# A softmax over eight dilated positions: logits copied out of PSUM in bf16, and one more chunk whose tiles are added before the logits

## The chip, the cores and the metric

The kernel runs on one core of one Trainium2 chip. The metric is the device time of one execution in microseconds. Before the change it is 208.17 us, the median of three runs (208.12 to 208.2). The execution that the profiler recorded took 208.24 us, of which the span from its first to its last instruction is 206.1 us.

## The reference

The inputs are a sequence `x` of 2048 rows by 640, and the weights of two branches that both read the normalised `x` and are added to it:

```
xn  = layernorm(x)                                  # no gain, no bias
out = x + A(xn) + B(xn)

A: q, k, v = xn @ wqkv, as 32 heads of 20
   row s looks at rows s, s-2, s-4, ... s-14        # W = 8 positions, dilation 2
   logits = q . k[those rows] / sqrt(20);  -1e9 where the row would be before 0
   o = softmax(logits over the 8) weighted sum of v[those rows]
   A = o @ wo
B: gelu(xn @ w1 + b1) @ w2 + b2                     # hidden width 1536
```

All inputs and the output are bf16.

## The kernel before, in words

The 2048 rows are taken as four chunks of 512 rows (chunk 0 to 3). Everything is kept with features on the partitions and rows along the free dimension, so a chunk of q, k or v is five tiles (t = 0 to 4) of 128 features by 512 rows.

For each chunk:

- ScalarE (ACT) or VectorE (DVE) normalise the rows (`xn`), and TensorE or a transposing DMA turns them (`tp`/`tc`).
- TensorE projects q, k and v (`hj` in chunk 0, `pj` in the others: five matmuls of 512 columns for each tile) and ACT copies each result out of PSUM (`hc`, `pc`). All projections and the first layer of branch B (`f1`) take their PSUM banks from one pool of four buffers, `psA`. A matmul group can begin only when the buffer it gets was emptied by ACT.
- VectorE multiplies q with the shifted k (`qk`, L429) for the eight positions, in two half tiles of four positions each (`half[0]`, `half[1]`), a chunk in four instructions: pair (of 256 rows) by half.
- The 20 products of a head have to be added. TensorE does that with a matrix of zeros and ones, `head_of` (`lg`, L475), in groups of four matmuls, one for each 128 rows, each of which fills 32 of the 128 partitions of `L`. How much VectorE adds beforehand is set by `LEVEL`: at 0 all five feature tiles go to TensorE (40 matmuls), at 1 VectorE first adds tiles 1 and 3 to tiles 0 and 2 (`pa`, L461, four instructions for a chunk) and 24 matmuls are left, at 3 `pb` (L466) adds the rest and 8 are left. Before, `LEVEL = (1, 0, 3, 3)` for the four chunks.
- Softmax (`PARTS` says that chunk 0 is done in two halves of 64 columns, a and b): `m` takes the maximum of the eight positions straight from PSUM (L516), `mx` subtracts it (L522, in f32), `ex` takes the exponential on ACT into the bf16 tile `e` (L532), `ss` adds the eight by halving (4+4, 2+2, 1+1, in f32; L536 and L538), `ri` takes the reciprocal on ACT by a logarithm and an exponential, `at` multiplies (L550) with the f32 reciprocal. In chunk 0 a mask is added first (L486).
- DMAs on the SyncE (SP) queue spread the weights from 32 heads to the partitions (`xd`, `xs`, L569); VectorE weights v (`av`, L584) and adds the eight (`ad`, `ot`).
- TensorE multiplies with w2 and wo (`t` pieces 0 to 3 for w2 and 4 for wo in chunks 0 to 2; `o` in chunk 3), ACT empties (`u`), SP turns (`ut`) and GpSimd (POOL) adds the result to `out` in HBM with an accumulating DMA (`ud`). The rows of `x` themselves are written to `out` before (`xp`, L298): chunk 0 from SP, chunks 1 and 2 from ACT. For chunk 3 they are added on VectorE (`xl`, `dl`, `dh`).

ACT needs one table set for the exponential and the logarithm and another for gelu; every switch is an instruction (L170).

The order of the work on TensorE, VectorE, ACT and SP is written out by hand: `ORDER` lists the pieces by the names above, and each engine runs its own pieces in that order and waits only for the data and the buffers that a piece needs. A name is read as kind, chunk, and the rest: `pj113` is chunk 1, k (0 is q, 2 is v), tile 3; `qk011` chunk 0, pair 1, half 1; `pa011` chunk 0, half 1, columns 256 to 511; `f10_7` chunk 0, tile 7; `t004` chunk 0, output tile 0, part 4. A PSUM buffer that was released earlier in `ORDER` is taken again by a later piece.

Of the kernel before, what the change touches and what calls it, by code (L numbers as in the profile page):

```python
# [37 lines left out]

ORDER = """
pad01 pad02 st00a st00 sum1 rs00 mean1 neg1 sq1 xn00a xn00b tp00a wa tp00b wb tc00a tc00b rs01 ga xn01a xn01b gb2  # L40
tp01a gb3 tp01b tc01a tc01b gb4 gd gc0 ge hj101 st02a tb st03a st02 rs02 st03 ho xn02 tp02 rs03 xn03 b1 st10a st12a
st11a st13a st12 st13 gc4 gc1 tc02 tp03 tc03 hj100 hc100 hj102 st11 hc101 hc102 pk hj010 hc010 hj112 st10 rs1 hc112
rc1 xn12 qk000 xn10 hj111 hc111 tc12 tc10 hj011 hc011 hj201 hc201 hj110 hj012 qk001 hc012 hc110 qk010 xn11 tc11 xn13
pa000 hj210 hj202 hc202 hj200 tc13 hc210 ldx ld2 ldo hc200 f10_0 f10_7 ge0_7 f10_10 f10_4 pj113 ge0_4 ge0_0 pj112
pj104 qk011 ge0_10 pc104 pj111 pc113 pa010 pc111 pa001 pj103 pc112 pa011 lg0 mask m0a mx0a pad11 pc103 su22 ex0a pj100
pc100 pj102 pc102 m0b mx0b ex0b ss0a ri0a ss0b pj114 pc114 at0a ri0b pj101 pc101 at0b xs0 xd0 pj110 pc110 qk100 qk101
qk110 f10_2 ge0_2 f10_9 hj212 su23 hc212 f10_1 qk111 su20 ge0_1 f11_0 ge0_9 su21 ge1_0 ng2 f10_5 f10_6 ge0_6 f11_5
ge1_5 sq23 ge0_5 f11_10 hj211 hc211 f10_3 pj121 lg1 av020 xp0 ge1_10 m1 sq21 ge0_3 av000 pj120 sq22 sq20 rs2 rc2 t040
t041 mx1 pc120 av010 xn22 av001 pc121 xn23 ex1 t000 pj123 tc22 av021 tc23 av031 av011 av030 ss1 f10_11 pj122 pc122
ad00 t001 f10_8 ge0_8 xn21 tc21 f11_9 ge0_11 xn20 tc20 pc123 t002 f11_2 xp1 t042 t043 f11_7 ge1_2 ge1_7 f11_8 ge1_9  # L50
ri1 at1 xp2 pad12 ad01 ad02 ot0 pj124 pc124 t003 pj211 pc211 su33 pj223 pc223 pj212 pj202 pc212 xd1 av111 su30 pj201
av110 pc201 av100 av101 pc202 su32 pj214 pc214 pj224 xs1 av121 av120 av131 pc224 av130 pj204 pc204 pj203 t004 su31
t044 u00 ng3 pad21 u04 t030 sq32 pj213 sq30 sq31 sq33 rs3 rc3 pc213 t031 t032 t033 t010 t011 t012 t013 ut00 ud00 pj200
pc200 t014 u01 pj210 pc210 xn31 tc31 t020 xn33 tc33 pc203 f12_8 t021 ge2_8 pad22 ad11 t022 t023 t034 u03 ad10 xn32
t024 ad12 ot1 f12_9 xn30 ge2_9 f12_11 pj222 pc222 qk201 qk200 qk211 f11_1 ge2_11 ge1_1 f11_3 qk210 tc32 f12_3 ge1_3
tc30 pj300 pc300 pj302 pc302 ut01 ud01 u02 f11_4 ge1_4 pj312 ge2_3 pa211 t100 pa201 pj322 pc322 ge1_8 pa200 pj310
pc310 pj314 pa210 pc312 pj303 pad31 pc303 pj304 pj320 pc314 pc320 pj313 pc313 pj311 pc311 f11_6 pj301 ge1_6 f13_4 t101
pb202 t102 pb212 pb204 pb214 lg2 ut02 f13_7 pc304 pc301 qk300 ge3_7 ut03 f11_11 m2 pa300 ge1_11 mx2 f13_1 ge3_1 t103
t104 u10 ex2 qk311 ss2 ri2 pa311 f13_10 t120 t121 at2 pj221 pc221 f13_8 ge3_4 qk310 t122 t123 t124 t140 t141 t142
ge3_8 f12_7 u12 pj321 pc321 pj324 pc324 xs2 xd2 ge3_10 qk301 ut04 ut10 pj220 t110 t143 f13_0 ge3_0 t111 f12_5 pj323  # L60
ge2_5 f12_10 pc220 ud02 pc323 pa301 pa310 pb302 pb312 pb304 pb314 f13_5 lg3 ge2_10 av220 ud10 f13_11 pad32 ge3_11
ge3_5 m3 mx3 t112 t113 t114 av210 ex3 t144 ss3 u11 av230 f12_0 ut11 ut12 ri3 at3 av201 f13_9 av231 av200 f12_2 t130
ge3_9 u14 t131 ud03 ge2_7 ge2_2 av221 av211 t132 t133 f13_2 ge3_2 f13_6 o300 ge2_0 t134 ad21 ud04 ad20 f13_3 ge3_3
ad22 f12_4 ge2_4 ot2 xd3 av311 f12_1 ge2_1 f12_6 t210 u13 ut13 ge2_6 xs3 av330 av300 ud11 ut14 ud12 ud13 o320 o321
ge3_6 o322 t200 t211 t201 t202 o301 o302 t203 t204 u20 ut20 ud20 av331 t212 t213 t214 t220 o310 u21 ut21 t221 t222
t223 t224 u22 ut22 o311 t230 av310 o312 o313 av301 ud21 ud22 t231 t232 t233 av321 av320 ad30 t234 o303 u23 ut23 t240
t241 t242 t243 t244 u24 o330 o331 o332 o333 ad31 o323 ad32 ot3 o324 o314 o304 xl0 o334 ohi xl1 dl2 ud14 dh2 dl1 dh1
dl0 dh0 ut24 ud23 dl3 dd1 dd2 dd0 dlo dh3 ud24 dhi
""".split()


# [1 line left out]
def kernel(  # L73
# [221 lines left out]

    def do_xp(n):
        cs, dst = rows(n)
        (nc.scalar if n else nc.sync).dma_start(dst, x_sb[:, cs, :])  # L298
# [197 lines left out]
    scratch = half[0][:].rearrange("p w t c -> p (w t c)").bitcast(F32)

    def shifted(n, i):
        if PARTS[n] == 1:
            return tiles["L", n][:]  # L500
        return scratch[:, 0 : W * P].rearrange("p (i w c) -> p i w c", i=PARTS[n], w=W)[:, i, :, :]
# [4 lines left out]
    def sums(n, i):

        if PARTS[n] == 1:
            return attn_tile(n)[:].rearrange("p w c -> p (w c)").bitcast(F32).rearrange("p (w c) -> p w c", w=W // 2)
        room = scratch[:, W * P : W * P + W * P // 2]  # L510
        return room.rearrange("p (i w c) -> p i w c", i=PARTS[n], w=W // 2)[:, i, :, :]

    def do_max(n, i):
        cs, width = part(n, i)
        m = softmax_tile("m", n, [P], F32)
        nc.vector.tensor_reduce(  # L516
            out=m[:, i, :], in_=tiles["L", n][:, :, cs].rearrange("p w c -> p c w"), axis=AX.X, op=ALU.max
        )

    def do_sub(n, i):  # L520
        cs, width = part(n, i)
        nc.vector.tensor_tensor(  # L522
            out=shifted(n, i),
            in0=tiles["L", n][:, :, cs],
            in1=tiles["m", n][:, i, :].unsqueeze(1).to_broadcast([P, W, width]),
            op=ALU.subtract,
        )

    def do_exp(n, i):
        e = softmax_tile("e", n, [W, P], BF16)  # L530
        table(LOG_SET)
        nc.scalar.activation(e[:, i, :, :], shifted(n, i), ACT.Exp, scale=SCALE)  # L532

    def do_sum(n, i):
        a, e = sums(n, i), tiles["e", n][:, i, :, :]
        nc.vector.tensor_tensor(out=a, in0=e[:, 0 : W // 2, :], in1=e[:, W // 2 :, :], op=ALU.add)  # L536
        for k in (2, 1):
            nc.vector.tensor_tensor(out=a[:, 0:k, :], in0=a[:, 0:k, :], in1=a[:, k : 2 * k, :], op=ALU.add)  # L538
# [311 lines left out]
```

## Time and profile before

| | before |
|---|---|
| median of 3 runs (lowest, highest) | 208.17 us (208.12, 208.2) |
| the profiled execution, and its span | 208.24 us, 206.1 us |
| TensorE matmul (PE), busy | 201.9 us, 98% of the span, 1148 instructions |
| VectorE (DVE), busy | 187.1 us, 91%, 162 instructions |
| ScalarE (ACT), busy | 125.0 us, 61%, 228 instructions |
| GpSimd (POOL), busy | 20.9 us, 10% |
| granted TensorE clock | 1.0 |
| DMA | 22.90 MB, mean 111 GB/s |

A busy share is an average over the span; whether an engine sets the time is read from the chain of work that ended last and from the waits. Matmuls overlap each other, so the length of one (379 ns for 512 columns) is not what it adds to the time.

### The profile page before, as it was taken

Reading aid. Unit: us, or ns where it says so; the run is one execution under the profiler, and the core shown is the slowest. Engines: PE = TensorE matmul, PEld = TensorE weight load, DVE = VectorE, ACT = ScalarE, POOL = GpSimd, SP = SyncE. Lnnn points to the kernel's source line nnn. Section 1 sums busy time; section 2 is a strip of 40 time slices with the busy share of each in tenths; the row PEclk is TensorE's granted clock in tenths of the full one; section 3 lists DMA queues with packets and bytes.
Section 4 is the critical chain, followed back from the end, with each engine's and each line's share of the span. In section 5 each row is a group of like instructions: output and inputs, shape, how many; then the busy total and the mean of one; then the engine's idle time right before and its main releaser. Section 6 shows DMA issues by size and latency. Waiting matters only on the chain.

```text
span 206.1 us, 2934 instructions
## 1 busy us (share of the span) xinstructions
PE 201.9 (98%) x1148; PEld 106.2 (52%) x1148; DVE 187.1 (91%) x162; ACT 125.0 (61%) x228; POOL 20.9 (10%) x33
## 2 busy tenths in 40 slices
PE   8999999999999999999999999999999999999994
PEld 3899654545444554444455544444444454444452
DVE  2989995998799999999999969999799999999953
ACT  5688959999897977859655536563488360211100
POOL 2000000000000000200014000001304002332220
PEclk9999999999999999999999999999999999999999
DMA  6996499194026281404437100066706619495543
GB/s 210 392 397 182 74 361 410 57 194 135 0 64 191 101 194 39 50 1 67 91 35 75 17 3 0 0 99 156 54 0 90 114 32 138 51 81 54 56 53 127
DMA packets 36063, 22.90 MB, mean 111 GB/s; under 512 B 24914, under 2 KB 33874, under 8 KB 36050
## 3 DMA queue, kind: packets, MB, share of 16 engines
q1 hardware_dynamic: 26752, 19.24, 34.8%
q0 software_dynamic: 7920, 1.97, 14.0%
q10 hardware_dynamic: 1378, 1.51, 2.0%
q8 instruction: 9, 0.15, 0.3%
q14 instruction: 4, 0.03, 0.1%
HBM read 10.00 MB, written 4.59 MB: 71 GB/s over the span
## 4 chain that ended last, share of the span: by engine, by line
PE 96%; DMA 1%; ACT 1%; DVE 0%; issue 0%
PE T L687 27%; PE hps L605 25%; PE pps L332 24%; PE gps L376 7%; PE lo L643 5%; PE L L475 2%; PE both L643 2%; PE gps L345 1%; PE hi L643 1%; DMA x_sb<-in_A_x_dram 1%; PE tp L277 1%; ACT trash L218 0%; DVE xn L262 0%; ACT logv L242 0%; DVE half L655 0%; ACT rstd L245 0%
## 5 line engine op out<-in xcount | busy, mean ns | idle before, releaser
L605 PE MATMUL hps<-xnT,w_sb 128*128 128x512 bf16 x240 | 55.9, 379 | 0.0
L429 DVE TENSOR_TENSOR half<-qT,kT 128x5120 bf16<-128x5120 bf16 x16 | 44.4, 2819 | 2.3 <-PE L L475 2.0
L687 PE MATMUL T<-hT,w_sb 128*128 128x512 bf16 x180 | 43.4, 379 | 0.0
L605 PEld LDWEIGHTS <-w_sb 128*128 128x128 bf16 x240 | 23.3, 98 | 27.9 <-issue 0.8
L699 POOL DMA_DIRECT2D out_dram<-x_sb x15 | 19.4, 1329 | 177.3 <-DMA x_sb<-x_sb 176.3
L687 PEld LDWEIGHTS <-w_sb 128*128 128x128 bf16 x180 | 17.4, 98 | 20.4
L621 ACT ACTIVATE hT<-hps,bT 128x512 bf16<-128x512 f32 x36 | 24.0, 687 | 6.3 <-PE hps L605 6.3
L584 DVE TENSOR_TENSOR half<-vT,ax 128x2560 bf16<-128x2560 bf16 x16 | 23.0, 1483 | 2.9 <-ACT trash L225 1.6
L690 ACT ACTIVATE x_sb<-T,bT 128x512 bf16<-128x512 f32 x15 | 10.3, 686 | 25.0 <-PE T L687 25.0
L584 DVE TENSOR_TENSOR half<-vT,x_sb 128x2560 bf16<-128x2560 bf16 x16 | 22.6, 1482 | 0.0
L593 DVE TENSOR_TENSOR half<-half,half 128x5120 bf16<-128x5120 bf16 x8 | 22.3, 2820 | 0.1
L332 PE MATMUL pps<-xnT,wv_sb 128*128 128x512 bf16 x75 | 18.3, 379 | 0.0
L687 PE MATMUL T<-oT,wo 128*128 128x512 bf16 x75 | 18.1, 379 | 0.0
L332 PE MATMUL pps<-xnT,wk_sb 128*128 128x512 bf16 x75 | 18.1, 379 | 0.0
L332 PE MATMUL pps<-xnT,wq_sb 128*128 128x512 bf16 x75 | 17.9, 379 | 0.0
L170 ACT ACT_TABLE_LOAD x12 | 15.4, 1283 | 0.9 <-PEq L834 0.7
L461 DVE TENSOR_TENSOR half<-half 128x2048 bf16<-128x2048 bf16 x12 | 14.1, 1217 | 0.0
L396 ACT CAST qT<-pps 128x512 bf16<-128x512 f32 x15 | 8.4, 582 | 7.4 <-PE pps L332 7.4
L332 PEld LDWEIGHTS <-wv_sb 128*128 128x128 bf16 x75 | 8.7, 118 | 7.8 <-issue 0.4
L332 PEld LDWEIGHTS <-wq_sb 128*128 128x128 bf16 x75 | 8.7, 118 | 7.7 <-issue 0.4
L332 PEld LDWEIGHTS <-wk_sb 128*128 128x128 bf16 x75 | 8.8, 117 | 7.5
L396 ACT CAST vT<-pps 128x512 bf16<-128x512 f32 x15 | 8.6, 582 | 6.2 <-PE pps L332 6.1
(94 smaller groups left out, 234.6 us busy)
## 6 DMA issues: line engine op xcount, KB each, us to landing
w_sb<-in_B_w_dram SPq DMA_DIRECT2D x4, 960.0 KB, 10.7
ax<-attn SPq DMA_DIRECT2D x8, 256.0 KB, 4.9
x_sb<-attn SPq DMA_DIRECT2D x8, 256.0 KB, 4.7
out_dram<-x_sb POOLq DMA_DIRECT2D x15, 128.0 KB, 3.9
x_sb<-in_A_x_dram SPq DMA_DIRECT2D x1, 1280.0 KB, 7.4
out_dram<-x_sb ACTq DMA_DIRECT2D x2, 640.0 KB, 3.2
wq_sb<-in_A_wqkv_dram SPq DMA_DIRECT2D x1, 800.0 KB, 4.8
wk_sb<-in_A_wqkv_dram SPq DMA_DIRECT2D x1, 800.0 KB, 6.7
```

The costliest lines, as they stand in the source:

```text
L170: nc.scalar.preload_act_table_set(name)
L332: nc.tensor.matmul(ps[:], lhsT=wqkv_p[which][:, ti, to, :], rhs=xnT[:, ti, :], start=(ti == 0), stop=(ti == KT - 1),)
L376: nc.tensor.matmul(ps[:, to - a, :], lhsT=wqkv_p[which][:, ti, to, :], rhs=tiles["xnT", 0][:, ti, pair * 2 * P : (pair + 1) * 2 * P], star ...
L396: nc.scalar.copy(dest[:, to, off : off + CH], tiles["pps", n, which, to][:])
L429: nc.vector.tensor_tensor(out=half[h][:, :, :, cs], in0=q[:, :, at].unsqueeze(1).to_broadcast([P, W // 2, KT, 2 * P]), in1=window(k, h, at ...
L584: nc.vector.tensor_tensor(out=half[h][:, :, :, cs], in0=window(qkv_tile(n, 2), h, cs), in1=ax_view(n)[:, j, ws, :].unsqueeze(2).to_broadca ...
L593: nc.vector.tensor_tensor(out=a, in0=a, in1=b, op=ALU.add)
L605: nc.tensor.matmul(ps[:], lhsT=w1_sb[:, ti, ft * P : (ft + 1) * P], rhs=tiles["xnT", n][:, ti, :], start=(ti == 0), stop=(ti == KT - 1),)
L621: nc.scalar.activation(hT, tiles["hps", n, ft][:], ACT.Gelu_apprx_tanh, bias=bT[:, ft : ft + 1], scale=1.0)
L643: nc.tensor.matmul(out_ps(bl, hi), lhsT=lhs, rhs=rhs[:, CH:D] if hi else rhs[:, 0:CH], start=pc == 0 and k == 0, stop=pc == 4 and k == len ...
L687: nc.tensor.matmul(ps[:], lhsT=lhs, rhs=rhs, start=pc == 0 and k == 0, stop=pc == 4 and k == len(srcs) - 1)
L699: nc.gpsimd.dma_start(dst, src, accum_op=ALU.add)
```

## The change

- `LEVEL` becomes (1, 1, 3, 3): chunk 1 gets four `pa` instructions on VectorE, and its logits 24 matmuls instead of 40.
- New pieces `cp` copy the logits from PSUM to the bf16 tile `e`: in chunk 0 columns 0 to 63 on ACT (`cp0a`) and 64 to 127 on VectorE (`cp0b`), in chunks 1 to 3 positions 0 to 3 and 4 to 7 (`cp1a`, `cp1b` and so on), both on ACT.
- The mask, the maximum (now by halving, three instructions), the subtraction and the weighting read and write bf16 in SBUF; the exponential works in place on `e`; the reciprocal is stored in bf16. The sum stays in f32.
- All three `xp` are issued from SP; in the new order they stand before `xs0` (`xp0`) and behind `xd0` (`xp1`, `xp2`).
- `ORDER` is another one throughout.

```diff
-LEVEL = (1, 0, 3, 3)
+LEVEL = (1, 1, 3, 3)
...
     def do_xp(n):
         cs, dst = rows(n)
-        (nc.scalar if n else nc.sync).dma_start(dst, x_sb[:, cs, :])
+        nc.sync.dma_start(dst, x_sb[:, cs, :])
...
+    def do_cp(n, i):
+        e = softmax_tile("e", n, [W, P], BF16)
+        if PARTS[n] == 1:
+            ws = slice(W // 2 * i, W // 2 * (i + 1))
+            nc.scalar.copy(e[:, 0, ws, :], tiles["L", n][:, ws, :])
+        else:
+            cs, width = part(n, i)
+            (nc.vector.tensor_copy if i else nc.scalar.copy)(e[:, i, :, :], tiles["L", n][:, :, cs])
+
     def do_mask():
-        L = tiles["L", 0]
-        nc.vector.tensor_tensor(out=L[0:H, :, 0:MW], in0=L[0:H, :, 0:MW], in1=mask[:], op=ALU.add)
+        e = tiles["e", 0][0:H, 0, :, 0:MW]
+        nc.vector.tensor_tensor(out=e, in0=e, in1=mask[:], op=ALU.add)
+
+    def fold(a, e, op):
+        nc.vector.tensor_tensor(out=a, in0=e[:, 0 : W // 2, :], in1=e[:, W // 2 :, :], op=op)
+        for k in (2, 1):
+            nc.vector.tensor_tensor(out=a[:, 0:k, :], in0=a[:, 0:k, :], in1=a[:, k : 2 * k, :], op=op)
 
     def do_max(n, i):
-        nc.vector.tensor_reduce(
-            out=m[:, i, :], in_=tiles["L", n][:, :, cs].rearrange("p w c -> p c w"), axis=AX.X, op=ALU.max
-        )
+        fold(room(n, i, BF16, 0), tiles["e", n][:, i, :, :], ALU.max)
 
     def do_sub(n, i):
...
-            out=shifted(n, i), in0=tiles["L", n][:, :, cs],
-            in1=tiles["m", n][:, i, :].unsqueeze(1).to_broadcast([P, W, width]), op=ALU.subtract,
+        e = tiles["e", n][:, i, :, :]
+        m = room(n, i, BF16, 0)[:, 0, :].unsqueeze(1).to_broadcast([P, W, width])
+        nc.vector.tensor_tensor(out=e, in0=e, in1=m, op=ALU.subtract)
 
     def do_exp(n, i):
-        nc.scalar.activation(e[:, i, :, :], shifted(n, i), ACT.Exp, scale=SCALE)
+        nc.scalar.activation(e, e, ACT.Exp, scale=SCALE)
 
     def do_sum(n, i):
+        fold(room(n, i, F32, W // 2 * P), tiles["e", n][:, i, :, :], ALU.add)
 
     def do_recip(n, i):
-        rs = get(("rs", n), lambda: smp.tile([P, PARTS[n], P // PARTS[n]], F32, tag="m", name="rs"))
+        rs = softmax_tile("rs", n, [P], BF16)
```

The part of the new `ORDER` from the logits of chunk 0 to those of chunk 1 and somewhat on:

```
... lg0 pc112 su20 cp0b cp0a m0b mask pj111 mx0b ex0b m0a pj114 pc114 ss0b mx0a pj101 pc101 ri0b pj113 pc113 ex0a pc111
pj100 at0b pc100 ss0a su22 qk111 ri0a qk101 pj124 pc124 at0a qk110 pa111 qk100 pa110 pa101 f11_3 pa100 f11_10 ge1_3 ldo
f10_8 ge0_8 hj210 hc210 xp0 su21 f10_2 ge0_2 su23 ge1_10 f10_0 ng2 ge0_0 f10_7 f10_3 f10_4 sq22 ge0_3 ge0_7 f11_5 sq21
ge0_4 sq23 f10_6 ge0_6 pj121 xs0 sq20 rs2 t040 t041 f11_0 rc2 pj122 pc122 xn22 pc121 xd0 xp1 xp2 tc22 xn23 tc23 lg1 cp1a
f10_10 f11_1 ge1_1 ge1_0 xn21 av020 cp1b ge0_10 t000 t001 t042 t002 xn20 f10_9 av030 av000 f11_9 ge1_9 av001 av011 tc21
f11_11 ge0_9 tc20 ge1_5 m1 av021 mx1 ex1 av031 pj120 ...
```

More of the change, by code (lines that the diff above doesn't have):

```diff
@@ L40 @@
 pad01 pad02 st00a st00 sum1 rs00 mean1 neg1 sq1 xn00a xn00b tp00a wa tp00b wb tc00a tc00b rs01 ga xn01a xn01b gb2
[L41 to L68, printed above, removed]
+tp01a gb3 tp01b tc01a tc01b gb4 gd gc0 ge st03a st02a tb hj100 st03 rs03 st02 xn03 b1 rs02 xn02 st11a st13a st10a st13
@@ new lines @@
+st12a st10 st12 st11 gc4 gc1 tp03 tc03 tp02 tc02 ho hj101 hc101 hj102 hc102 hj011 hc100 hc011 rs1 hj112 hc112 rc1 xn12
+tc12 qk000 hj012 qk001 hj201 xn10 tc10 hc012 hc201 hj211 hc211 hj110 hc110 hj010 hc010 f10_1 pk pa000 xn13 hj111 tc13
+xn11 tc11 ldx ld2 pa010 hc111 qk010 hj212 qk011 pa001 pa011 hc212 f10_5 f10_11 ge0_11 ge0_1 hj200 ge0_5 hc200 hj202
+pj103 pc103 pj104 pc104 pad11 pj110 pc110 pj102 pc102 pj112 hc202 lg0 pc112 su20 cp0b cp0a m0b mask pj111 mx0b ex0b
+m0a pj114 pc114 ss0b mx0a pj101 pc101 ri0b pj113 pc113 ex0a pc111 pj100 at0b pc100 ss0a su22 qk111 ri0a qk101 pj124
@@ new lines @@
+pc124 at0a qk110 pa111 qk100 pa110 pa101 f11_3 pa100 f11_10 ge1_3 ldo f10_8 ge0_8 hj210 hc210 xp0 su21 f10_2 ge0_2
+su23 ge1_10 f10_0 ng2 ge0_0 f10_7 f10_3 f10_4 sq22 ge0_3 ge0_7 f11_5 sq21 ge0_4 sq23 f10_6 ge0_6 pj121 xs0 sq20 rs2
+t040 t041 f11_0 rc2 pj122 pc122 xn22 pc121 xd0 xp1 xp2 tc22 xn23 tc23 lg1 cp1a f10_10 f11_1 ge1_1 ge1_0 xn21 av020
+cp1b ge0_10 t000 t001 t042 t002 xn20 f10_9 av030 av000 f11_9 ge1_9 av001 av011 tc21 f11_11 ge0_9 tc20 ge1_5 m1 av021
+mx1 ex1 av031 pj120 pc120 t003 pj123 pc123 t043 pad12 av010 pj221 pc221 ss1 pj224 ri1 ad01 at1 pc224 pj220 pj200 su33
@@ new lines @@
+pc220 ad00 ad02 ot0 pc200 pj214 pc214 xs1 su32 av131 pj202 pc202 pj213 pc213 pad21 pj212 pc212 su31 pj204 pj210 pc210
+pc204 av121 pj211 pj203 pj201 su30 ng3 sq32 sq30 t004 u00 t044 u04 sq31 pc211 xd1 av101 av100 av111 av120 av130 sq33
+ut00 t010 ud00 t011 t012 t013 t014 pc201 av110 u01 rs3 rc3 pj222 pc203 pad22 ad10 t030 t031 f11_6 xn32 tc32 t032 ad11
+ad12 t020 t021 t022 xn30 tc30 f11_2 pc222 ge1_2 t023 t033 t034 xn33 tc33 t024 ge1_6 ot1 f11_4 qk201 qk200 qk210 xn31
+ge1_4 qk211 pa200 pa211 pa201 u03 pa210 pb202 pb212 pb204 pj223 f12_1 pc223 f11_8 ge1_8 f12_6 ut01 ge2_6 ge2_1 pb214
@@ new lines @@
+t130 tc31 pj310 pc310 pj303 pc303 pj301 pc301 ge1_11 f11_7 pj311 pc311 pj302 pj312 pc302 pj313 pc312 ge1_7 pc313 u02
+ut02 pj300 f13_3 f12_10 pc300 pj322 pc322 pj320 pc320 pj304 ge2_10 ut03 ut04 ud01 pad31 pc304 pj314 pc314 ud02 ge3_3
+f13_9 f12_7 ge3_9 ge2_7 lg2 cp2b qk310 cp2a m2 mx2 f13_5 ge3_5 qk311 f13_2 pj324 pc324 pj321 ex2 ss2 pa311 t131 t132
+t133 ri2 at2 xd2 t140 t134 ud03 pc321 u13 ge3_2 f13_7 t141 t142 t143 f13_4 f13_0 t100 ge3_7 t101 f12_11 ge2_11 pj323
+t102 t103 qk300 f13_6 t104 ge3_6 f13_10 ge3_10 ge3_0 t144 u14 f12_0 ge3_4 pc323 ge2_0 qk301 xs2 pa300 pa310 pa301
@@ new lines @@
+pb312 pb302 pb314 f13_1 pb304 lg3 xl0 cp3a cp3b av230 ge3_1 av201 m3 av210 pad32 t110 f12_3 f12_2 t111 t112 mx3 t113
+t114 u10 ut10 ex3 f12_8 f12_9 o300 av200 ss3 u11 ut11 av220 ri3 at3 av231 t120 av211 av221 o301 ud10 t121 t122 ge2_3
+t123 f13_8 ge2_2 ge3_8 ge2_9 ad21 ad20 t124 xd3 xs3 ad22 u12 ut12 ot2 av321 av331 f12_5 f13_11 ge3_11 f12_4 ge2_5 t230
+o310 ge2_4 av320 t231 ge2_8 t232 o320 av330 av311 av300 av310 av301 ad30 t200 ud11 t233 t201 t202 t203 o321 ud04 t204
+ut13 ut14 u20 ut20 t234 ad31 u23 t210 t211 t212 t213 ud12 t214 t220 u21 t221 o322 t222 t223 t224 u22 o311 o330 o312
@@ L69 @@
+ud13 o313 ud20 o302 t240 ut21 t241 t242 t243 o323 t244 o331 o303 o332 o333 ad32 ot3 o324 xl1 o314 o304 dl2 ud14 dh2
+dl1 u24 o334 dh1 dl0 ohi ud21 ut22 ud22 ut23 ut24 dd2 dd1 dh0 dd0 dl3 dh3 dhi dlo ud23 ud24
 """.split()
@@ L482, in do_lg @@
                     )
-    def do_mask():
-        L = tiles["L", 0]
-        nc.vector.tensor_tensor(out=L[0:H, :, 0:MW], in0=L[0:H, :, 0:MW], in1=mask[:], op=ALU.add)
     def part(n, i):
@@ L494, in softmax_tile, with room @@
         return get((key, n), lambda: smp.tile([P, PARTS[n]] + [s // PARTS[n] if s == P else s for s in shape], dtype, tag=key, name=key))
[L496 to L501, printed above, removed]
+    scratch = half[0][:].rearrange("p w t c -> p (w t c)")
     def attn_tile(n):
         return get(("attn", n), lambda: smp.tile([P, W, P], BF16, tag="attn", name="attn"))
-    def sums(n, i):
+    def room(n, i, dtype, off):
+        size = W // 2 * P // PARTS[n] * (2 if dtype == F32 else 1)
@@ L508, in sums @@
         if PARTS[n] == 1:
-            return attn_tile(n)[:].rearrange("p w c -> p (w c)").bitcast(F32).rearrange("p (w c) -> p w c", w=W // 2)
-        room = scratch[:, W * P : W * P + W * P // 2]
-        return room.rearrange("p (i w c) -> p i w c", i=PARTS[n], w=W // 2)[:, i, :, :]
-    def do_max(n, i):
-        cs, width = part(n, i)
-        m = softmax_tile("m", n, [P], F32)
-        nc.vector.tensor_reduce(
-            out=m[:, i, :], in_=tiles["L", n][:, :, cs].rearrange("p w c -> p c w"), axis=AX.X, op=ALU.max
-        )
+            flat = attn_tile(n)[:].rearrange("p w c -> p (w c)")[:, 0:size]
+        else:
+            flat = scratch[:, off + i * size : off + (i + 1) * size]
@@ new lines, in room, with do_mask @@
+        return flat.bitcast(dtype).rearrange("p (w c) -> p w c", w=W // 2)
+    def do_cp(n, i):
[3 more added lines that the diff above has]
+            nc.scalar.copy(e[:, 0, ws, :], tiles["L", n][:, ws, :])
+        else:
+            cs, width = part(n, i)
+            (nc.vector.tensor_copy if i else nc.scalar.copy)(e[:, i, :, :], tiles["L", n][:, :, cs])
+    def do_mask():
+        e = tiles["e", 0][0:H, 0, :, 0:MW]
+        nc.vector.tensor_tensor(out=e, in0=e, in1=mask[:], op=ALU.add)
@@ L520, in do_sub @@
+    def fold(a, e, op):
+        nc.vector.tensor_tensor(out=a, in0=e[:, 0 : W // 2, :], in1=e[:, W // 2 :, :], op=op)
+        for k in (2, 1):
+            nc.vector.tensor_tensor(out=a[:, 0:k, :], in0=a[:, 0:k, :], in1=a[:, k : 2 * k, :], op=op)
+    def do_max(n, i):
+        fold(room(n, i, BF16, 0), tiles["e", n][:, i, :, :], ALU.max)
     def do_sub(n, i):
         cs, width = part(n, i)
[L522 to L527, printed above, removed]
+        e = tiles["e", n][:, i, :, :]
+        m = room(n, i, BF16, 0)[:, 0, :].unsqueeze(1).to_broadcast([P, W, width])
+        nc.vector.tensor_tensor(out=e, in0=e, in1=m, op=ALU.subtract)
@@ L529, in do_exp @@
     def do_exp(n, i):
-        e = softmax_tile("e", n, [W, P], BF16)
+        e = tiles["e", n][:, i, :, :]
         table(LOG_SET)
-        nc.scalar.activation(e[:, i, :, :], shifted(n, i), ACT.Exp, scale=SCALE)
+        nc.scalar.activation(e, e, ACT.Exp, scale=SCALE)
     def do_sum(n, i):
[L535 to L538, printed above, removed]
+        fold(room(n, i, F32, W // 2 * P), tiles["e", n][:, i, :, :], ALU.add)
@@ L540, in do_recip @@
     def do_recip(n, i):
-        rs = get(("rs", n), lambda: smp.tile([P, PARTS[n], P // PARTS[n]], F32, tag="m", name="rs"))
-        total = sums(n, i)[:, 0, :]
+        rs = softmax_tile("rs", n, [P], BF16)
+        total = room(n, i, F32, W // 2 * P)[:, 0, :]
         table(LOG_SET)
@@ L779 @@
         piece(f"lg{n}", do_lg, n)
+        for i in range(2):
+            piece(f"cp{n}" + "ab"[i], do_cp, n, i)
         for name, fn in (("m", do_max), ("mx", do_sub), ("ex", do_exp), ("ss", do_sum), ("ri", do_recip), ("at", do_attn)):
```

## The prediction

> **What bounds the kernel now.** I read the totals, then the chain of work that ended last, then the waits, and only then the prices of single instructions. First the page's own lines (busy times; the ACT row of the 40 slices, in tenths; the chain by engine):
>
> ```profile
> span 206.1 us, 2934 instructions
> ...
> PE 201.9 (98%) x1148; PEld 106.2 (52%) x1148; DVE 187.1 (91%) x162; ACT 125.0 (61%) x228; POOL 20.9 (10%) x33
> ...
> ACT  5688959999897977859655536563488360211100
> ...
> PE 96%; DMA 1%; ACT 1%; DVE 0%; issue 0%
> ```
>
> TensorE is the chain. VectorE is nearly as full, and ScalarE is full in the first 85 us. The chain in order of time (start, length, what) shows that it is not merely busy:
>
> ```profile
> 31.99 1.41 PE L L475 x24
> ...
> 41.08 0.55 PE gps L376 x5
> ...
> 49.19 1.08 PE hps L605 x5
> ...
> 51.35 2.27 PE L L475 x40
> ...
> 62.81 0.65 PE T L687 x3
> ...
> 121.52 0.55 PE L L475 x8
> ...
> 147.64 0.55 PE L L475 x8
> ...
> 202.08 0.96 PE hi L643 x17
> 203.06 0.29 DVE half L655
> ```
>
> From the first projections to 203 us each piece starts where the last one stops; in the waits no PE line of the middle of the kernel appears. Five matmuls of 512 columns add 1.08 us, three 0.65 us, five of 256 columns 0.55 us. So the time is the sum of matmul work plus a start and a tail, and two things count: what TensorE has to do, and whether a new order leaves it waiting.
>
> **TensorE.** Chunk 1's logits go from 40 matmuls to 24. Chunk 0 has run 24 already: 1.41 us against 2.27 us. That removes 0.86 us of the chain; nothing else on TensorE changes in number or shape. (By 16 equal shares of the 2.27 us it would be 0.91 us; I take the row.)
>
> **VectorE.** The rows by shape (the last two numbers before the bar are count and busy time, then the mean ns of one):
>
> ```profile
> L461 DVE TENSOR_TENSOR half<-half 128x2048 bf16<-128x2048 bf16 x12 | 14.1, 1217 | 0.0
> ...
> L522 DVE TENSOR_TENSOR L<-L,m 128x1024 f32<-128x1024 f32 x3 | 3.7, 1226 | 0.0
> L516 DVE TENSOR_REDUCE m<-L 128x128 f32<-128x1024 f32 x3 | 3.7, 1217 | 0.0
> L550 DVE TENSOR_TENSOR attn<-e,rs 128x1024 bf16<-128x1024 bf16 x3 | 3.6, 1217 | 0.0
> ...
> L655 DVE TENSOR_TENSOR half<-lo,x_sb 128x512 bf16<-128x512 f32 x3 | 2.1, 692 | 1.9 <-PE lo L643 1.9
> ...
> L536 DVE TENSOR_TENSOR attn<-e 128x512 f32<-128x512 bf16 x3 | 2.0, 682 | 0.0
> ...
> L302 DVE TENSOR_TENSOR x_sb<-x_sb,b2bc 128x1280 bf16<-128x1280 bf16 x2 | 1.6, 817 | 0.0
> L522 DVE TENSOR_TENSOR half<-L,m 128x512 f32<-128x512 f32 x2 | 1.4, 691 | 0.1
> L550 DVE TENSOR_TENSOR attn<-e,rs 128x512 bf16<-128x512 bf16 x2 | 1.4, 688 | 0.0
> ...
> L538 DVE TENSOR_TENSOR attn<-attn 128x256 f32<-128x256 f32 x3 | 1.3, 425 | 0.1
> ...
> L538 DVE TENSOR_TENSOR attn<-attn 128x128 f32<-128x128 f32 x3 | 0.9, 292 | 0.1
> ...
> L538 DVE TENSOR_TENSOR half<-half 128x64 f32<-128x64 f32 x2 | 0.5, 225 | 0.1
> ```
>
> All-bf16 rows give 2048 elements in 1217 ns and 1280 in 817: 0.52 ns for each element and about 150 ns besides. L550 is the telling one: with one f32 operand 1024 elements take those same 1217 ns. So I estimate for all-bf16 operations 684 ns (1024), 417 (512), 284 (256), 217 (128), 183 (64); the upper ends are the f32 rows of equal size.
>
> - Chunks 1 to 3, each: the maximum by halving 417 + 284 + 217 = 918 ns against 1217; the subtraction 684 against 1226; the weighting 684 against 1217. Together 1.37 us less. At f32 prices (682 + 425 + 292 for the halving) 0.2 us more.
> - Chunk 0, each half: halving 284 + 217 + 183 = 684, about what it was; subtraction and weighting 0.27 us less each. Added: `cp0b`, 512 elements out of PSUM, 0.42 to 0.69 us, taken at 0.69 (L655 is nearest).
> - Chunk 1: four `pa`, 4 × 1.217 = 4.87 us more.
>
> In all -4.1 - 1.1 + 0.7 + 4.9 = +0.4 us on VectorE. The total costs nothing by itself; what counts is whether VectorE is in time where TensorE takes its results.
>
> **ScalarE.** Seven copies of 512 columns out of PSUM come on top, at the price of the casts it does now; the 13 instructions of the densest stretch are summed with these rows (time line and groups):
>
> ```profile
> 35.76 1.05 ACT L396 CAST qT<-pps 128x512 bf16<-128x512 f32 x2
> ...
> 39.95 1.28 ACT L170 ACT_TABLE_LOAD   x1
> 41.24 0.69 ACT L621 ACTIVATE hT<-hps,bT 128x512 bf16<-128x512 f32 x1
> ...
> 62.01 0.42 ACTq L298 DMA_DIRECT2D out_dram<-x_sb  x1
> ```
> ```profile
> L621 ACT ACTIVATE hT<-hps,bT 128x512 bf16<-128x512 f32 x36 | 24.0, 687 | 6.3 <-PE hps L605 6.3
> ...
> L260 ACT ACTIVATE xn<-x_sb,nmr,rstd 128x640 bf16<-128x640 bf16 x12 | 10.6, 916 | 0.9 <-DVE nmr L250 0.9
> ...
> L532 ACT ACTIVATE e<-half 128x512 bf16<-128x512 f32 x2 | 1.3, 636 | 0.4 <-DVE half L522 0.4
> ```
>
> Two casts take 1.05 us, so one behind another adds about 0.48; in the same way a gelu adds 0.58, an `xn` 0.82, a table load 1.29. The number of table loads stays. Copies 7 × 0.48 = 3.4 us, less the issue of two transfers (0.42 each), over the whole kernel.
>
> **Where TensorE could wait: the logits of chunk 1.** VectorE now has 4.9 us more ahead of `lg1`, which stands later in the order. VectorE's rows:
>
> ```profile
> 15.62 8.29 DVE L429 TENSOR_TENSOR half<-qT,kT 128x5120 bf16<-128x5120 bf16 x3
> 23.83 1.22 DVE L461 TENSOR_TENSOR half<-half 128x2048 bf16<-128x2048 bf16 x1
> 24.97 2.82 DVE L429 TENSOR_TENSOR half<-qT,kT 128x5120 bf16<-128x5120 bf16 x1
> ...
> 121.94 2.83 DVE L429 TENSOR_TENSOR half<-qT,kT 128x5120 bf16<-128x5120 bf16 x1 [1.99 <-PE L L475]
> ...
> 142.22 4.62 DVE L466 TENSOR_TENSOR half<-half 128x2048 bf16<-128x2048 bf16 x4
> ...
> 172.85 1.49 DVE L598 TENSOR_TENSOR oT<-half 128x2560 bf16<-128x2560 bf16 x1
> ```
>
> A `qk` adds (23.83 - 15.62)/3 = 2.74 us, a `pa` 24.97 - 23.83 = 1.14.
>
> TensorE: ahead of `lg0` stand one `f1` (1.08) and `hj210` (1.10) fewer, `hj211` (1.10) and `hj212` (0.55) more, so `lg0` runs from 31.99 - 0.53 = 31.46 to 32.87. VectorE has chunk 0's four `qk` and four `pa` done at 15.62 + 10.95 + 4.56 = 31.13: no wait. From `lg0` to `lg1` TensorE has 19 groups of 1.08, `hj210` and two of 0.65: `lg1` is due at 32.87 + 20.52 + 1.10 + 1.30 = 55.79.
>
> VectorE from 32.87: `cp0b` to 33.56, `m0b` 34.25, mask 34.47, `mx0b` 34.89, `m0a` 35.57; `ex0b` on ScalarE ends at 34.89 + 0.64 = 35.53, so `ss0b` (425 + 292 + 225 ns) ends at 36.5, `mx0a` at 36.93. Then ScalarE rules: `ex0a` is queued behind `pc113`, whose matmuls end four groups after `lg0`, at 37.19; `pc113` to 37.77, `ex0a` 38.41, and behind it `pc111` and `pc100`, to about 39.5. `ss0a` ends at 39.35, and `qk111` needs `pc100`: 39.5. Four `qk`, four `pa` and `at0a` (0.35): 39.5 + 10.95 + 4.56 + 0.35 = 55.4. Against 55.79 that leaves 0.4 us. At the upper prices `mx0a` ends 1.04 us later, of which 0.84 disappear in the wait for `pc113`; with `at0a` 0.5 us late in all, a wait of 0.1.
>
> **PSUM buffers behind it.** `rc2` stands behind `pa100` on VectorE, and `xn22`, with all of ScalarE's queue, behind `rc2`. From 55.79, when `pj122` ends: `pc122`, `pc121`, `cp1a`, `cp1b` 1.92, four `xn` 3.28, a table load 1.29, `ge1_1`, `ge1_0`, `ge0_10` 1.74, `ge1_9` 0.58: 8.8 us, to 64.6, which frees the buffer that I take `pj120` to get. `pj120` is due after `lg1` (1.41), two `f1`, four `t` parts, three `f1`: 55.79 + 1.41 + 2.16 + 2.60 + 3.24 = 65.2. Cover 0.6 us. `cp1a` waits for `lg1` in that queue, but is reached only after the `lg1` matmuls have ended.
>
> **Later hand-overs.** `lg2` to `lg3`: before, VectorE began 0.42 us after `lg2` (121.94 against 121.52), ended at 146.84 and was 0.8 us ahead of 147.64. After, VectorE has 24.9 - 1.4 = 23.5 us, TensorE thirteen groups of 1.08, eleven of 0.65, three of 1.08 and 0.55, together 25.0: 1.1 us ahead. `ot2` ended at 174.34, ahead of `t204`, for which I count 27.2 us of TensorE work from 147.64: 0.5 us ahead. After, both lose about 1.4 us: the cover is again 0.5. From `ot2` to `ot3` no operation changes.
>
> **SyncE.** `xp1` and `xp2` now stand between `xd0` and the transposes of chunk 2, and `xp0` ahead of `xs0`. SyncE's row:
>
> ```profile
> 43.96 0.60 SPq L298 DMA_DIRECT2D out_dram<-x_sb  x1
> ```
>
> Three times 0.6 us of issue; chunk 0's weights (`at0a` at 45.3) are used after 55.4, and `xn22` isn't there before 57: hidden on both sides by several us, and without that cover 0.6 us each.
>
> **The sum.** The profiled execution's 208.24 us is its span of 206.1 and 2.14 around it; the median is 0.07 lower. 208.17 - 0.86 = **207.3 us** with every wait covered. About 0.2% (0.42 us) is what a measurement of this kernel can tell from no change, so two thirds of the gain must reach the end to be 207.75 or less.
>
> **The rivals.**
>
> 1. *The covers leak (same).* Those I found are 0.4 to 0.6 us, thinner than the errors of sums over twenty rows. Waits of 0.45 to 1.28 us in all give 207.75 to 208.6. For it: ScalarE's nines up to 85 us; against: the order before had covers of 0.5 to 0.8 us and no wait. 0.14.
> 2. *The matmuls removed were free (same).* If the four groups run beside each other so well that 16 fewer save nothing: 208.2. Against it stand 1.41 and 2.27 us in the chain. 0.03.
> 3. *ScalarE becomes the bound between 55 and 66 us (slower).* It is the one place where VectorE's new work, ScalarE's new copies and the PSUM pool meet: everything waits for `rc2`. ScalarE late by d makes TensorE wait d - 0.6 for a buffer at `pj120`. From d = 1.9 (0.6 + 0.86 + 0.42) the kernel is slower; with 0.2 us more for each of its 13 instructions d is 2.6 and the time 209.3. For it: the queue has no idle time in my sum. Against: its rows are those of instructions that run there today. 0.13.
> 4. *The bf16 forms run at one element a cycle (slower).* VectorE then pays 1.55 us more in each of chunks 1 to 3 than I took: waits of 0.1 at `lg1`, 0.45 at `lg3`, 1.05 at `ot2`: 208.9; it decides from about 1.4 us more for each. Against: L461, in place, and L429, with a repeated operand, run at two. 0.05.
> 5. *Table loads drain (same).* If a load cost 1.38 us more than its row, ScalarE would be that late at `pj120`, and the time 207.3 + 0.8 = 208.1. The rows say no: the gelu starts 1.29 us after its load began. 0.02. The Trainium skill's "ScalarE: Activation LUTs" ("What ACT_TABLE_LOAD costs") states a drain of about 1380 ns behind the load's 1283 ns; the trace has the 1283 and not the drain, so by that rule the kernel would land at rival 5, and I don't follow it.
>
> **How the numbers follow.** The forecast has 0.63; rivals 1, 2 and 5 make "same" 0.19, rivals 3 and 4 "slower" 0.18. The range begins at 207.0 (0.3 under the forecast, for 0.91 in place of 0.86 and the scatter of single pieces) and reaches over the "same" cases to 208.6, leaving out the slower 0.18.
>
> **What would show it.** Right: `L` in chunk 1 as 24 matmuls in about 1.4 us; no idle time of PE before L332, L475 or L687; L550's successor near 684 ns; VectorE's total within 1 us of 187. Wrong: PE waiting for ACT in front of projections near 65 us (rival 3), or for DVE in front of `L` or of the first `T` part with wo (rivals 1 and 4).

## The result, and the profile after

| | before | after |
|---|---|---|
| median, first comparison | 208.16 us (4 runs) | 207.1 us (4 runs, 206.87 to 207.37) |
| ratio, 95% interval | | 0.9949 [0.9932, 0.9967] |
| ratio of a second comparison, on its own chip | | 0.9948 [0.9935, 0.9960], median 206.98 us |
| profiled execution, its span | 208.24 us, 206.1 us | 207.11 us, 205.2 us |

The kernel is 0.5% faster, 1.06 us by the medians; 207.3 us was forecast. The page after, lines as shown of before:

```profile
span 205.2 us, 2907 instructions
...
PE 199.6 (97%) x1113; PEld 105.5 (51%) x1132; DVE 187.2 (91%) x177; ACT 127.8 (62%) x235; POOL 20.9 (10%) x33
...
ACT  5689967999899887859655576571775650211100
...
PE 95%; DMA 1%; ACT 1%; issue 1%; DVE 0%
```

VectorE's total moved by 0.1 us although four additions came on, ScalarE's by 2.8. TensorE is still the chain. TensorE's own total can't be compared here: 1113 of the 1132 matmuls that run are in this trace (a second one, of the same kernel, has all 1132 and 201.3 us), and the pieces whose records are missing make up the "issue 1%". The chain in order of time, at the places shown of before:

```profile
31.44 1.41 PE L L475 x24
...
55.87 1.41 PE L L475 x24
...
65.37 1.08 PE pps L332 x5
...
123.64 0.55 PE L L475 x8
...
148.69 0.55 PE L L475 x8
...
201.18 0.96 PE hi L645 x17
202.17 0.29 DVE half L657
```

Chunk 1's logits take 1.41 us in place of 2.27, and the last matmul group begins at 201.18 in place of 202.08: 0.90 us earlier, the 0.86 and next to nothing else. The rest of the 1.06 us, some 0.2 to 0.3, lies outside the span (see the last point on the prediction). In the list of waits no PE line names another engine for the middle of the kernel. The new VectorE instructions by shape (mean ns behind the comma):

```profile
L532 DVE TENSOR_TENSOR e<-e,attn 128x1024 bf16<-128x1024 bf16 x3 | 2.1, 687 | 0.0
...
L552 DVE TENSOR_TENSOR attn<-e,rs 128x1024 bf16<-128x1024 bf16 x3 | 2.1, 684 | 0.0
...
L521 DVE TENSOR_TENSOR attn<-e 128x512 bf16<-128x512 bf16 x3 | 1.3, 421 | 0.0
...
L523 DVE TENSOR_TENSOR attn<-attn 128x256 bf16<-128x256 bf16 x3 | 0.9, 292 | 0.1
...
L523 DVE TENSOR_TENSOR attn<-attn 128x128 bf16<-128x128 bf16 x3 | 0.7, 225 | 0.1
```

Each is within 10 ns of its estimate (684, 684, 417, 284, 217); the copy of 512 elements out of PSUM took 0.69 us, in a row shown further down.

### The profile page after: what moved, and what is told of

Read it like the earlier page. It is cut to its first block, busy times and chain, and to the rows that moved or that the text cites. A ratio compares the mean times of both kernels' runs of the same rounds, so it can differ in the third digit from the quotient of the medians.

```text
span 205.2 us, 2907 instructions
## 1 busy us (share of the span) xinstructions
PE 199.6 (97%) x1113; PEld 105.5 (51%) x1132; DVE 187.2 (91%) x177; ACT 127.8 (62%) x235; POOL 20.9 (10%) x33
## 4 chain that ended last, share of the span: by engine, by line
PE 95%; DMA 1%; ACT 1%; issue 1%; DVE 0%
PE T L689 27%; PE hps L607 25%; PE pps L332 24%; PE gps L376 7%; PE lo L645 5%; PE both L645 2%; PE L L475 2%; PE hi L645 2%; PE gps L345 1%; DMA x_sb<-in_A_x_dram 1%; PE tp L277 1%; ACT trash L218 0%; DVE xn L262 0%; ACT logv L242 0%; DVE half L657 0%
## 5 line engine op out<-in xcount | busy, mean ns | idle before, releaser
L607 PE MATMUL hps<-xnT,w_sb 128*128 128x512 bf16 x232 | 55.3, 379 | 0.4
L689 PE MATMUL T<-hT,w_sb 128*128 128x512 bf16 x179 | 42.7, 379 | 0.1
L461 DVE TENSOR_TENSOR half<-half 128x2048 bf16<-128x2048 bf16 x16 | 18.8, 1219 | 0.0
L260 ACT ACTIVATE xn<-x_sb,nmr,rstd 128x640 bf16<-128x640 bf16 x12 | 10.7, 918 | 2.9 <-DVE nmr L250 2.2
```

What stands on the lines that cost most here:

```text
L461: nc.vector.tensor_tensor(out=even, in0=even, in1=odd, op=ALU.add)
L607: nc.tensor.matmul(ps[:], lhsT=w1_sb[:, ti, ft * P : (ft + 1) * P], rhs=tiles["xnT", n][:, ti, :], start=(ti == 0), stop=(ti == KT - 1),)
L689: nc.tensor.matmul(ps[:], lhsT=lhs, rhs=rhs, start=pc == 0 and k == 0, stop=pc == 4 and k == len(srcs) - 1)
```

## The experiments

Three groups of kernels ran, each on its own chip beside runs of the kernel before (medians 208.12, 208.3 and 208.27 us); between groups the ratios are to be compared. Theory A throughout: the gain is the 16 matmuls, and everything else in the change makes room for VectorE's four additions without letting TensorE wait.

**The changed kernel again.**

> The changed kernel itself, as an anchor for the others of this chip: 207.1 us by every theory (its runs so far 206.9 to 207.4), and TensorE's last matmul near 202.1 us as in its first profile.

206.98 us, ratio 0.9948, the span again 205.2 us: the anchor holds.

**Chunk 1 back at level 0.**

```diff
-LEVEL = (1, 1, 3, 3)
+LEVEL = (1, 0, 3, 3)
```
with `pa100`, `pa101`, `pa110`, `pa111` out of `ORDER`.

> The changed kernel with chunk 1 at level 0: no adds ahead of its logits and 40 matmuls; order, bf16 softmax and x writes as changed. Theory A (the gain is the 16 matmuls, everything else only keeps TensorE from waiting): 0.86 us above the changed kernel, 207.95, and VectorE's 4.6 us less buy nothing. Theory B (the gain comes from the new order or the softmax): no difference, 207.1.

207.78 us, ratio 0.9981 [0.9972, 0.9990]: 0.80 us above the changed kernel. Its chain:

```profile
55.93 2.27 PE L L475 x40
...
202.10 0.96 PE hi L645 x17
```

The matmuls are what the span lost: with them back, the last group begins at 202.10, against 202.08 in the kernel before. Against B. But the time is still 0.34 us below the kernel before with the same span of 206.1 us; that remainder is followed below.

**The old softmax in the new order.**

On the kernel before:

```diff
-LEVEL = (1, 0, 3, 3)
+LEVEL = (1, 1, 3, 3)
-        (nc.scalar if n else nc.sync).dma_start(dst, x_sb[:, cs, :])
+        nc.sync.dma_start(dst, x_sb[:, cs, :])
```
with the new `ORDER` without the `cp` pieces.

> The changed kernel with the old softmax: maximum and subtraction in f32 straight from PSUM, no copies; level 1 in chunk 1, the new order without the copies, x writes from SyncE. Theory A (VectorE must be in time, and its covers are 0.2 us at chunk 1's logits, 1.0 at chunk 2's, 0.85 at chunk 3's, 0.5 at the attention output of chunk 2): 1.4 us more on VectorE for each of chunks 1 to 3 make TensorE wait about 0.1 + 0.5 + 0.5 + 0.9 us: 209.1. Theory B (VectorE has room, the bf16 softmax isn't needed): 207.1.

208.62 us, ratio 1.0027 [1.0016, 1.0038]: slower than before, with 16 matmuls fewer. Its time lines, TensorE and then VectorE:

```profile
55.78 1.48 PE L475 MATMUL L<-half,head_of 128*32 128x512 bf16 x24
...
123.55 0.79 PE L475 MATMUL L<-half,head_of 128*32 128x512 bf16 x8
...
149.15 0.61 PE L475 MATMUL L<-half,head_of 128*32 128x512 bf16 x8 [0.31 <-DVE half L466]
...
175.93 2.32 PE L687 MATMUL T<-oT,wo 128*128 128x512 bf16 x10 [0.83 <-DVE oT L598]
```
```profile
119.27 4.62 DVE L466 TENSOR_TENSOR half<-half 128x2048 bf16<-128x2048 bf16 x4
124.06 2.83 DVE L429 TENSOR_TENSOR half<-qT,kT 128x5120 bf16<-128x5120 bf16 x1 [0.17 <-PE L L475]
...
174.39 1.49 DVE L598 TENSOR_TENSOR oT<-half 128x2560 bf16<-128x2560 bf16 x1
```

The waits stand at chunk 3's logits and at the first product with chunk 2's attention output, as theory A had it. At chunk 2's logits a small one lies inside the group: VectorE's last addition ends at 119.27 + 4.62 = 123.89, after the group has begun, and the eight matmuls take 0.79 us where the changed kernel's take 0.62. At chunk 1's logits there is none: without the copies VectorE began its multiplications for chunk 1 at 39.42, 0.35 us earlier than with them. Against the changed kernel TensorE is 0.16 us late behind chunk 2's logits, 0.53 at chunk 3's (149.15 against 148.62 in the same view) and 1.53 at the attention output (175.93 against 174.40): about 1.5 us and not 2.0; the medians differ by 1.64. The bf16 softmax is needed, although alone it is worth nothing (next but two).

**The x writes back on ScalarE.**

```diff
-        nc.sync.dma_start(dst, x_sb[:, cs, :])
+        (nc.scalar if n else nc.sync).dma_start(dst, x_sb[:, cs, :])
```

> The changed kernel with the writes of x for chunks 1 and 2 issued by ScalarE again, at their new place in the order. Theory A (the move from ScalarE to SyncE is worth nothing): 207.0 to 207.2. Theory B (two issues of 0.42 us land in ScalarE's full stretch at 57 us, where a PSUM buffer comes free 0.3 us before TensorE needs it): up to 0.5 us more, 207.6.

207.19 us, ratio 0.9959 [0.9945, 0.9972] beside 0.9948 [0.9935, 0.9960]. The intervals overlap: if the move is worth anything it is some 0.2 us, which the times don't resolve. The chain in its trace shows where they come from:

```profile
57.34 4.58 DMA xnT<-xn
...
62.01 0.55 ACT xn L260
...
64.80 0.59 ACT hT L623
...
65.43 1.24 PE pps L332 x5
66.67 0.65 PE T L689 x3
```

The two issues (0.42 and 0.52 us) cost ScalarE nothing: they run beside its other work, and the normalisation behind the first begins at 56.40, against 56.39 in the changed kernel. But now the two writes of 640 KB move while chunk 2 is transposed. One transposing DMA lands after 4.6 us, where all four of the changed kernel take 2.4, ScalarE waits 0.34 us for it (until 62.01), and the gelu that frees `pj120`'s buffer ends at 65.39. TensorE takes the buffer at 65.43: the cover there is just used up, and what follows stands 0.22 us later (66.67 against 66.45). So theory B has the place and less than half of the size, but not the reason.

**The kernel before, once more.**

> The kernel before, unchanged, for a second profile of it: the changed kernel with 40 matmuls ended its span with the same 206.1 us as the first profile of the kernel before, and yet was 0.34 us faster in the comparison. Theory A (the 0.3 us lie outside the span and belong to single executions): span 206.1, and a time less span below the 2.14 us of the first profile. Theory B (the kernel before has a longer time outside its span): 2.1 us again.

Ratio 1.0009 [0.9982, 1.0036], as it should be. The profiled execution took 209.46 us with a span of 207.3 us; outside the span lie 2.16 us, as 2.14 in the first profile, and 2.1 to 2.2 us in all twelve executions. So theory B, in numbers. That span was longer for a reason at its very start:

```profile
1.20 6.28 DMA wq_sb<-in_A_wqkv_dram
...
7.53 1.03 PE gps L345 x15
...
203.31 0.96 PE hi L643 x17
```

The first weights landed late (6.3 us after their issue, 4.8 in the first profile), TensorE began its projections at 7.53 us, and everything up to the end was shifted by 1.2 us. A single execution of this kernel can differ by more than the change is worth, for a transfer in its first 8 us.

**The bf16 softmax alone, in the old order.** The new functions with `LEVEL = (1, 0, 3, 3)`, x writes from ScalarE, and the copies put into the old order where ScalarE is free:

```diff
-lg0 mask m0a mx0a pad11 pc103 su22 ex0a
+lg0 pad11 pc103 su22 cp0b cp0a mask m0a mx0a ex0a
-m1 sq21 ge0_3 av000 pj120 sq22 sq20
+sq21 ge0_3 av000 pj120 sq22 sq20 cp1a cp1b m1
...
```
with `cp2a cp2b` behind `pc301` and `cp3a cp3b` behind `pad32`.

> The kernel before with the bf16 softmax alone: its own order, with the copies put where ScalarE reaches them, level 0 in chunk 1, x writes from ScalarE as before. Theory A (TensorE doesn't wait in the kernel before, so a faster softmax on VectorE buys nothing): 208.0 to 208.2. Theory B (the softmax itself shortens the time): 207.6 or less. A third way: the two copies of chunk 1 wait for the logits in ScalarE's full queue ahead of the next normalisation: up to 1 us slower, 209.1.

208.49 us, ratio 1.0005 [0.9990, 1.0020]: no change, though VectorE was busy 183.2 us instead of 187.1. Two things cancel in this: the span of the profiled execution is 0.7 us longer than before (206.8 us), and the time outside it 0.3 us shorter (1.8 us in all executions). In the trace TensorE has one new wait, 0.36 us at 43.15 for a gelu on ScalarE. It isn't the third way: the chain that leads there begins with the copies of chunk 0, not of chunk 1 (`cp0b` at 33.54, `cp0a` behind it at 34.26, the mask at 34.88).

**The four additions alone, in the old order.**

```diff
-LEVEL = (1, 0, 3, 3)
+LEVEL = (1, 1, 3, 3)
-... f10_3 pj121 lg1 ...
+... f10_3 pj121 pa100 pa101 pa110 pa111 lg1 ...
```

> The kernel before with level 1 in chunk 1 alone: the four adds put in VectorE's order ahead of the logits, everything else as before. Theory A (the adds have to be hidden by an order with later logits): VectorE ends its multiplications 0.4 us before the logits are due, the adds take 4.6 us, so TensorE waits 4.2 us, gets 0.86 back and waits some 0.5 us more for the attention output of chunk 0: 212.0. Theory B (TensorE has slack there, the matmuls removed are the whole of it): 207.3.

210.99 us, ratio 1.0152 [1.0105, 1.0199], about 3 us slower: theory A's direction, less than its 3.9 us by the median (the interval reaches from 2.2 to 4.1 us). The profiled execution is one of the long ones, 212.38 us with a span of 210.5; four of the six took 210.74 to 211.14. The time line shows the logits of chunk 1 following the additions one at a time:

```profile
52.11 0.39 PE L475 MATMUL L<-half,head_of 128*32 128x512 bf16 x2 [0.83 <-DVE half L461]
53.25 0.82 PE L475 MATMUL L<-half,head_of 128*32 128x512 bf16 x10 [0.74 <-DVE half L461]
54.38 0.39 PE L475 MATMUL L<-half,head_of 128*32 128x512 bf16 x2 [0.31 <-DVE half L461]
55.52 1.47 PE L475 MATMUL L<-half,head_of 128*32 128x512 bf16 x10 [0.74 <-DVE half L461]
```

**The new order alone.** The kernel before with the new `ORDER`, from which the `cp` and the `pa1` pieces are taken out.

> The kernel before in the new order alone: old softmax, level 0 in chunk 1, x writes from ScalarE, the copies and the four adds left out of the order. Theory A (the new order hides work and shortens nothing): the 0.86 us of matmuls are back and the waits for the old softmax at the logits of chunk 3 and the attention output of chunk 2 stay as they were with 24 matmuls, 0.45 and 0.9 us: 209.2. Theory B (the new order by itself is worth 0.3 us): 207.8.

209.85 us, ratio 1.0064 [1.0040, 1.0089]: the order by itself makes the kernel 1.3 us slower by the ratio (1.1 expected), with VectorE late at the same places as under the old softmax:

```profile
PE T L687 <- DVE oT L598: 0.8, 1, 0.8
...
PE L L475 <- DVE half L466: 0.5, 1, 0.5
```

None of the three parts helps alone: +1.3 us, nothing, +3 us. Together they take 1 us away.

**VectorE made late.** In the changed kernel, one addition that nothing uses:

```diff
+    def do_xx(n):
+        nc.vector.tensor_tensor(out=spare[:], in0=half[0][:, :, n, :], in1=half[0][:, :, n, :], op=ALU.add)
-... pa101 f11_3 pa100 ...
+... pa101 f11_3 xx1 pa100 ...
```

> The changed kernel with one more VectorE instruction (an addition of 2048 bf16 elements that nothing uses, 1.22 us, 1.14 in a row) just ahead of the last add before the logits of chunk 1. Theory A (the cover there is the 0.2 us of the trace, and what exceeds it reaches the end): 0.95 us above the changed kernel, 207.95. Theory B (VectorE is busy 91% and so has room, a later wait takes it up): 207.0 to 207.1.

Ratio 0.9999 [0.9984, 1.0013], 0.0050 above the changed kernel's (which ran on other chips): 1.0 us, 0.95 expected. In the trace:

```profile
56.80 1.48 PE L480 MATMUL L<-half,head_of 128*32 128x512 bf16 x24 [1.01 <-DVE half L461]
```

The same behind `at3`:

> The same extra instruction, but behind the softmax of chunk 3, ahead of the attention output of chunk 2. Theory A (the cover there is 0.46 us): 0.7 us above the changed kernel, 207.7. Theory B (VectorE has room): 207.0 to 207.1.

Ratio 0.9979 [0.9963, 0.9995], 0.0030 above: 0.6 us, 0.7 expected.

```profile
175.34 2.32 PE L694 MATMUL T<-oT,wo 128*128 128x512 bf16 x10 [0.56 <-DVE oT L605]
```

(Of the 0.94 us by which this piece is later than the changed kernel's, at 174.40, 0.22 were there already at chunk 0's logits; the instruction accounts for 0.7.) Of 1.14 us about 0.15 and 0.45 are absorbed, and what exceeds them reaches the end. VectorE, off the chain and idle 9% of the span, has less than half a microsecond to give at these two places.

## Why the prediction was right

**TensorE's 0.86 us.** It was read from the pieces with 24 and 40 matmuls and came out as such: 2.27 to 1.41 us in the chain, 0.90 us at the last matmul, 0.80 us by the medians when it was undone. Rival 2 falls.

**The prices.** All-bf16 operations cost what the straight line through 2048 and 1280 elements gave, so rival 4 has no ground. VectorE's forecast of +0.4 us was +0.1. ScalarE's busy time rose by 2.8 us; the 3.4 us of its copies are what that compares with, because issues of transfers aren't counted as busy. The two issues that the prediction took off (0.42 us each) were no gain: with the writes back on ScalarE they delayed nothing there.

**The hand-overs.** `lg0` was forecast for 31.46 and began at 31.44, `lg1` for 55.79 and began at 55.87, `pj120` for 65.2 and began at 65.37. The cover of a hand-over is the time by which a result is ready before TensorE needs it. VectorE after, around the logits of chunk 0 and at the ends before a hand-over, with ScalarE's copy:

```profile
32.90 0.69 DVE L514 CAST e<-L 128x512 bf16<-128x512 f32 x1 [1.85 <-PE L L475]
...
36.18 0.42 DVE L521 TENSOR_TENSOR half<-e 128x256 f32<-128x256 bf16 x1 [0.64 <-ACT e L537]
...
39.77 5.56 DVE L429 TENSOR_TENSOR half<-qT,kT 128x5120 bf16<-128x5120 bf16 x2
...
52.19 3.49 DVE L461 TENSOR_TENSOR half<-half 128x2048 bf16<-128x2048 bf16 x3
...
143.22 4.63 DVE L466 TENSOR_TENSOR half<-half 128x2048 bf16<-128x2048 bf16 x4
...
172.45 1.49 DVE L600 TENSOR_TENSOR oT<-half 128x2560 bf16<-128x2560 bf16 x1
```
```profile
33.62 0.59 ACT L514 CAST e<-L 128x512 bf16<-128x512 f32 x1 [0.83 <-DVE e L514]
34.23 1.28 ACT L170 ACT_TABLE_LOAD   x1
35.52 0.63 ACT L537 ACTIVATE e<-e 128x512 bf16<-128x512 bf16 x1
...
37.68 0.57 ACT L396 CAST kT<-pps 128x512 bf16<-128x512 f32 x1
...
64.33 1.85 ACT L623 ACTIVATE hT<-hps,bT 128x512 bf16<-128x512 f32 x3
```

The covers were thinner than forecast: `pa100` ended at 55.68, 0.2 us ahead of `lg1` (0.4 forecast); the gelu that frees a buffer ended at about 64.33 + 0.69 = 65.02, 0.35 us ahead of `pj120` (0.6); chunk 2's additions ended at 147.85, 0.8 us ahead of `lg3` (1.1); `ot2` at 173.94, 0.5 us ahead of its use at 174.40 (0.5). None was used up, so rivals 1 and 3 didn't happen. They were real all the same: `xx1` and `xx3` exceed two of them and are paid for, and the x writes from ScalarE use up the one at `pj120`.

One step of the chain was wrong. I let `cp0a` on ScalarE run beside `cp0b` on VectorE. The rows show it waiting 0.83 us for `cp0b` (33.62), with the table load and `ex0b` behind it; `ss0b` waited 0.64 us for that. `ri0b`, which stands ahead of `pc113` on ScalarE, waited for `ss0b` in turn, so that `pc113` began at 37.68 and not at 37.19. By the time of `qk111` only 0.27 us of the delay were left (39.77 against 39.5), because the prediction had everything wait for `pc113` anyway.

**Table loads.** In the rows above the exponential begins 1.29 us after its table load began, as the gelu did in the kernel before (39.95 and 41.24): rival 5 falls. The drain in "ScalarE: Activation LUTs" of the Trainium skill ("What ACT_TABLE_LOAD costs") isn't to be seen here.

**The term that was missing: 0.2 to 0.3 us outside the span.** I carried 2.14 us outside the span over to the changed kernel. It has 1.8 to 1.9 there (207.11 - 205.2; the others 207.37 - 205.6, 206.87 - 205.1, 207.09 - 205.3, 206.96 - 205.2). The kernel with chunk 1 back at level 0 has 207.94 - 206.1 = 1.8, which is its remainder of 0.3 us. It is 1.8 us as well with the bf16 softmax alone, and 1.7 to 1.9 with the four additions alone, both in the old order; it is 2.0 to 2.1 with the new order alone, and 1.9 to 2.1 with the new order and the additions under the old softmax. So it goes with the program, and not with the matmuls, which are 40 with the bf16 softmax alone and 24 with the additions alone. What it is stays open: no view shows the time outside the span, and no experiment was made on it. About a quarter of the gain is therefore not what was forecast. The range held it.

## What to carry to other kernels

When one engine's chain has no gaps, count what is taken off that engine and read it from a group of the same kind in the same trace; then spend the effort on the hand-overs, summing the rows on each side in the new order. Faster work on an engine off the chain was worth nothing by itself here; it paid for work moved there, and only because the order lets the consumer come later. An average load says little of it: VectorE was idle 9% of the span and had 0.2 us to spare at the place that mattered.

## What the runs showed of the hardware

In the profiled execution of the four additions in the old order, TensorE spent about 4 us in short pieces between waits, and then worked at half its clock (stretches of 1 us: engine busy times, TensorE's first, and behind them the granted clock, PEclk):

```profile
53.00:54.00 1.00, 0.75 (x10) 0.23 (x10) 1.00 (x2) 0.98 (x3) 0.00 (x0) 1.00 0.00 0
54.00:55.00 1.00, 0.47 (x4) 0.10 (x2) 1.00 (x2) 0.99 (x2) 0.00 (x0) 0.97 0.00 0
55.00:56.00 1.00, 0.48 (x8) 0.24 (x9) 1.00 (x2) 0.30 (x2) 0.00 (x0) 0.50 0.00 0
56.00:57.00 1.00, 1.00 (x11) 0.16 (x4) 0.87 (x1) 0.00 (x0) 0.00 (x0) 0.50 0.00 0
57.00:58.00 1.00, 1.00 (x3) 0.37 (x4) 0.98 (x1) 0.00 (x0) 0.00 (x0) 0.50 0.00 0
58.00:59.00 1.00, 1.00 (x5) 0.43 (x4) 1.00 (x2) 0.10 (x1) 0.00 (x0) 0.83 0.00 0
```

The clock falls to 0.50 near 55 us and is back after 58, so here the wait is paid for a second time: this execution took 212.38 us, some 1.5 us more than the four at a mean clock of 1.0. The waits don't always bring it: of six executions two had a lower mean clock (0.992 here, 0.983 at 213.85 us). Nor are they needed for a lower mean: the kernel before had one execution at 0.992 (211.22 us). What decides stays open. With the single late addition, one wait of 1 us, the mean granted clock of the profiled execution was 1.0. The Trainium skill, "TensorE: Matmul & The Clock Gate" (Part 1), puts the return to half clock at an idle window of about 3.4 us, but also tells of a kernel in which short idle times between groups of matmuls were enough. Here it came after TensorE had been busy 0.75 and 0.47 of the two microseconds before.
